# Reciprocals taken on 128x8 and spread by ScalarE, with the attention's loads and copies stated later

## The chip, the cores and the metric

The kernel runs on one core of a Trainium2 chip. The metric is device time in microseconds (us) of one execution. Five engines work from instruction queues of their own, each in the order in which its queue stands: TensorE (PE, with its weight loads listed apart as PEld), VectorE (DVE), ScalarE (ACT), GpSimd (POOL) and SyncE (SP), which here only issues transfers (DMAs). An instruction whose inputs are not ready holds up everything behind it on its engine.

## The reference

```python
scores = scale * q @ k.T                       # per batch and head, 576 x 576
scores = where(causal, -1e9, scores); scores -= scores.max(-1)
a = exp(scores); a /= a.sum(-1) + 1e-09
local = a @ v
q_p = where(q > 0, q, exp(q) - 1) + 1
mem_out = (q_p @ M_prev) / (q_p @ z_prev + 1e-06)
g = 1 / (1 + exp(-beta))
x = g * mem_out + (1 - g) * local              # 4 batches x 8 heads x 576 x 64
x = x.transpose(0, 2, 1, 3).reshape(2304, 512)
r = relu(x @ w_in); x = (s * r * r + b) @ w_out          # 512 -> 2048 -> 512
h = x @ w2_in; z = h * softmax(h)                         # 512 -> 1024
x = (z - mean(z)) / sqrt(var(z) + 1e-06) * g_ln @ w2_out  # 1024 -> 512
```

The results are float32. The four weight matrices arrive as 64-bit floats, which the kernel reads as pairs of 32-bit words and "decodes" on the chip into a high and a low part.

## The kernel before, in words

The attention runs over 16 units `u` (4 batches x 4 pairs of heads). A unit has 4 full tiles of 128 query rows for each of the two heads and one shared tail tile, 9 tiles in 5 steps `i` (0 to 4; `CF` is 4). `scores` multiplies on PE, a DVE instruction (L336, L362) adds the mask, takes the row's minimum of the scaled scores (`mx`) and copies the tile to `pr`; ACT takes the exponential (L312) and sums the row into `sums`. Two steps later `transposes` turns `pr` over on PE (tiles `pp`, L377), and ACT copies it to `pt` (L383). `values` multiplies with `v` into the PSUM tile `po` (L411), adds the memory part `mq` x `Mb` (L416), and DVE scales `po` by `R` into `xb` (L418).

The division by the row sums is done by `weigh` and `recip_t`: the 8 row sums of a unit (4 tiles x 2 heads, a 128x8 tile) get 1e-9 added (L279); DVE takes the reciprocal of each, 64 times over, into `r` of 128x512 (L281); PE transposes `r` in four pieces (`tr`, L293), and ACT copies the result to `R` (L295). The product of `den` and `sums` (L283) weighs the memory part `ph`.

From unit 4 on the scores use a high and a low part: `split` makes `hi` of `kq` on ACT (L242, one buffer), the remainder on POOL (L243, in place), and eight copies by DMA put both into `sk` and `k2` (L249, L250). `load` brings in `kq`, `q`, `v` (two buffers each) and, at the first pair of a batch, `zb` and `Mb`. All these DMAs, the weights' loads (L147) and the stores stand in SP's one queue.

PE's spare time in the attention is filled with the first part of the MLP of finished batches (`first_part`, L430 to L432 and L471 to L473), and 11 weights are decoded meanwhile: ACT L152, DVE L153, L154, L156, L158, POOL L159, ACT L163, DVE L164. After the attention come the rest of that first part, the second part (`second_part`) and the second MLP (`mlp2`).

Nobody writes the order of the queues by hand. A scheduler lays out the queues from the order in which the program states its instructions: what is stated earlier goes first where two could go, and its own model of times decides when something could. To state a load or a copy later in the program is thus to give it a lower rank against what stands between.

Of the kernel before, what the change touches and what calls it, by code (L numbers as in the profile page):

```python
# [8 lines left out]
F32 = mybir.dt.float32  # L9
# [3 lines left out]
AF = mybir.ActivationFunctionType  # L13
# [4 lines left out]
P = 128  # L18
# [5 lines left out]
def attention_mlp_kernel(  # L24
# [9 lines left out]
    nc = tc.nc  # L34
    B, NPAIR, _, NCH, _, D = q.shape
    H = 2 * NPAIR
# [7 lines left out]
    CF = S // P  # L44
# [31 lines left out]
    def warm_up(n):  # L76

        ps = ps_m.tile([P, 512], F32, tag="m", name=f"warm{n}")
        for _ in range(n):
            nc.tensor.matmul(ps[:, 0:256], warm[:, 0:P], warm, start=True, stop=True)  # L80

    def load_gate():
        nc.sync.dma_start(gate, beta.partition_broadcast(P))
        nc.scalar.activation(gate, gate, AF.Exp, scale=-1.0)
        nc.vector.tensor_scalar(gate, gate, 1.0, None, ALU.add)
        nc.vector.reciprocal(gate, gate)
        nc.vector.tensor_scalar(omg, gate, -1.0, 1.0, ALU.mult, ALU.add)
        gg = gate.rearrange("p (a j) -> p a j", j=2)
        nc.vector.tensor_copy(gmt[0:64], gg[0:64, :, 0])
        nc.vector.tensor_copy(gmt[64:128], gg[64:128, :, 1])  # L90

    def load_consts():
        nc.sync.dma_start(s_sb, moe_s.partition_broadcast(P))
        nc.sync.dma_start(b_sb, moe_b.partition_broadcast(P))
        with nc.allow_non_contiguous_dma(reason="a small vector"):
            nc.sync.dma_start(gl_sb, g_ln.rearrange("(f p) -> p f", p=P))
# [78 lines left out]
    def decode_to(n):  # L175
        while decoded[0] < min(n, NW):
            with tc.issue_after(mark[0]) if mark[0] else nullcontext():
                decode(decoded[0])
            decoded[0] += 1


    NU = B * NPAIR

    QT = S + CF * P
    RL = QT + P
    NRAW = NPAIR
    xbs = {}

    class Attention:
# [16 lines left out]
            self.zb = {}  # L206
            self.tiles = [(i, j) for i in range(CF) for j in range(2)] + [(CF, None)]

        def load(self, u, names=("kq", "q", "v")):
            b, a = divmod(u, NPAIR)  # L210
            p = self.pair.setdefault(u, {})
            if "kq" in names:
                t = p["raw"] = self.ld.tile([P, RL], F32, tag="kq", name=f"kq{u}")
                nc.sync.dma_start(t, kq[b, a])
            for nm in "qv":
                if nm in names:
                    t = p[nm] = self.ld.tile([P, NCH, 2, D], F32, tag=nm, name=f"{nm}{u}")
                    nc.sync.dma_start(t, (q if nm == "q" else v)[b, a])
            if a == 0 and "v" in names:
                self.zb[b] = self.st.tile([P, H, D], F32, tag="zb", name=f"zb{b}", bufs=1)  # L220
                nc.sync.dma_start(self.zb[b], z_prev[b].partition_broadcast(P))
                for j in range(2):
                    nc.sync.dma_start(self.Mb[b % 2][j * D:(j + 1) * D, :, j * D:(j + 1) * D],
                                      M_prev[b].rearrange("(a j) d e -> j d a e", j=2)[j])

        def gates(self, u):

# [45 lines left out]
        def weigh(self, u):  # L273


            p = self.pair[u]
            sums, den, ph = p.pop("sums"), p.pop("den"), p["ph"]
            sv = sums[:, 0:CF].rearrange("p c h -> p (c h)")
            nc.vector.tensor_scalar(sv, sv, 1e-9, None, ALU.add)  # L279
            r = p["r"] = self.st.tile([P, CF * 2, D], F32, tag="r", name=f"r{u}", bufs=1)  # L280
            nc.vector.reciprocal(r, sv.unsqueeze(2).to_broadcast([P, CF * 2, D]))  # L281
            dv = den.rearrange("p c h -> p (c h)")
            nc.vector.tensor_tensor(dv, dv, sums.rearrange("p c h -> p (c h)"), ALU.mult)  # L283
            nc.gpsimd.tensor_tensor(ph.rearrange("p c h d -> p (c h) d"), ph.rearrange("p c h d -> p (c h) d"),
                                    dv.unsqueeze(2).to_broadcast([P, NCH * 2, D]), ALU.mult)

# [197 lines left out]
    def load2(bi, part=None):  # L484
        t0, n = blocks[bi]
        if part is not True:
            x = xq[bi] = xs2.tile([P, NC, NB], F32, tag="x", name=f"xr{bi}")
            nc.sync.dma_start(x[:, :, 0:n], xd[:, :, t0:t0 + n])
        if part is not False:
            nc.sync.dma_start(yT[:, :, t0:t0 + n], yd[:, :, t0:t0 + n])  # L490

    pctx = ctx.enter_context(ExitStack())
    with ExitStack() as fctx:
        xp = fctx.enter_context(tc.tile_pool(name="xp", bufs=2))
        xs = fctx.enter_context(tc.tile_pool(name="xs", bufs=1))
        gs = fctx.enter_context(tc.tile_pool(name="gs", bufs=FP1 + 1))
        ys = fctx.enter_context(tc.tile_pool(name="ys", bufs=2))
        ps_m = fctx.enter_context(tc.tile_pool(name="ps_m", bufs=2, space=PSUM))
        fpools = [xs, gs, ys, [ps_m]]
        filler = []  # L500
        with ExitStack() as actx:
            at = Attention(actx, xp)
            NS = CF + 1
            G = NU * NS
            at.load(0, ("kq",))
            warm_up(16)
            load_gate()
            at.load(1, ("kq",))
            at.load(0, ("q", "v"))
            at.phi(0)  # L510
            at.load(1, ("q", "v"))
            load_consts()
            LAG = 2
            FG = NPAIR * NS + LAG + 1
            debt = 0.0
            tiles_of = lambda i: (2 * i, 2 * i + 1) if i < CF else (2 * CF,)
            for g in range(G + LAG):
                u, i = divmod(g, NS)
                if g < G:
                    for t in tiles_of(i):  # L520
                        at.scores(u, t)
                if g < 4:
                    with tc.issue_after(at.last):
                        warm_up(6)
                if i == 0 and NRAW <= u + 1 < NU:
                    at.split(u + 1)
                if i == 0 and u + 2 < NU:
                    at.load(u + 2)
                if i == 2 and 0 < u < NU:
                    at.phi(u)  # L530
                if i == 3 and u < NU:
                    at.gates(u)
                if i == CF and u < NU:
                    at.weigh(u)
                if 0 <= g - LAG:
                    lu, li = divmod(g - LAG, NS)
                    for t in tiles_of(li):
                        at.transposes(lu, t)
                    if li == CF - 1:
                        at.recip_t(lu)  # L540
                        at.phi_t(lu)
                    if li == CF:
                        at.values(lu)
                        if lu % NPAIR == NPAIR - 1:
                            filler.append(first_part(lu // NPAIR, fpools))
                decode_to(min(int(g / 3.4), RA))
                if filler and g >= FG:
                    debt += 0.93 * 6 * (FP1 + NC) / (G - FG)
                    while debt >= 1 and filler:
                        debt -= 1  # L550
                        if next(filler[0], 0) == 0:
                            filler.pop(0)
        wpools[1] = ctx.enter_context(tc.tile_pool(name="wpB", bufs=RB, side="right", reuse_waits="tile"))
        xs2 = pctx.enter_context(tc.tile_pool(name="xs2", bufs=1, side="right", reuse_waits="tile"))
        gs2 = pctx.enter_context(tc.tile_pool(name="gs2", bufs=2, side="right", reuse_waits="tile"))
        ps_y = pctx.enter_context(tc.tile_pool(name="ps_y", bufs=1, side="right", space=PSUM, reuse_waits="tile"))
        ps_h = pctx.enter_context(tc.tile_pool(name="ps_h", bufs=2, side="right", space=PSUM, reuse_waits="tile"))
        fpools[3] = [ps_h, ps_m]
        load2(0, False)
        attended[0] = True  # L560
        for it in filler:
            for _ in it:
                decode_to(min(decoded[0] + 1, RA + RB))
# [198 lines left out]
```

## Time and profile before

| what | value |
|---|---|
| median of 3 runs | 941.71 us (938.75 to 942.41) |
| profiled execution, own time | 937.02 us |
| its span (what the rows cover) | 935.2 us |
| PE busy | 876.7 us (94%) |
| DVE busy | 627.6 us (67%) |
| ACT busy | 453.0 us (48%) |
| POOL busy | 217.3 us (23%) |
| mean granted PE clock | 0.983 of full speed |

Busy shares are averages over stages that differ: the attention takes about the first 384 us, the rest of the first part and the second part follow to some 600 us, then the second MLP. PE's busy time counts a pipelined matmul from its start to a modelled end, so a PE that is busy is not always at its peak; PEld gives the weight loads beside it.

### The profile page before, as it was taken

How to read it: one execution, taken by the hardware profiler on the slowest of the kernel's cores; microseconds unless marked ns; L12 is line 12 of the kernel's file. 1: busy time of each engine (PE TensorE's matmuls, PEld its weight loads, DVE VectorE, ACT ScalarE, POOL GpSimd, SP SyncE). 2: the span in 40 equal slices, each digit the busy share in tenths (PEclk: the TensorE clock that was granted, in tenths of full speed). 3: DMA queues.
4: the chain of work that ended last, by engine and by line, in shares of the span. 5: the costliest groups of instructions: out<-in, count | busy, mean ns of one | idle time of the engine just before them, and what ended most of it. 6: DMA issues, size and time to landing. Idle time of an engine off the chain costs nothing.

```text
span 935.2 us, 13612 instructions
## 1 busy us (share of the span) xinstructions
PE 876.7 (94%) x5008; PEld 706.2 (76%) x5008; DVE 627.6 (67%) x1251; ACT 453.0 (48%) x1008; POOL 217.3 (23%) x176
## 2 busy tenths in 40 slices
PE   8897878899999899799989999999999999999997
PEld 5444655887887787698767888889877888888886
DVE  5977899677676867699897633243898645444442
ACT  4665676556666666455345332233443533333332
POOL 5334435233333322143340300000232100000000
PEclk9989799999999999999999999999999999999999
DMA  8339757565656550345833200010140000000000
GB/s 241 101 112 245 199 152 182 152 186 153 179 133 182 130 135 13 112 161 158 305 106 98 90 6 18 1 46 2 45 136 23 12 23 23 22 23 23 23 23 34
DMA packets 46530, 93.69 MB, mean 100 GB/s; under 512 B 7808, under 2 KB 21120, under 8 KB 46464
## 3 DMA queue, kind: packets, MB, share of 16 engines
q1 hardware_dynamic: 46464, 92.83, 34.4%
q8 instruction: 39, 0.64, 0.3%
q14 instruction: 27, 0.22, 0.1%
HBM read 56.63 MB, written 14.16 MB: 76 GB/s over the span
## 4 chain that ended last, share of the span: by engine, by line
PE 61%; DVE 17%; DMA 9%; issue 5%; ACT 3%; SPq 3%; POOL 1%; ACTq 0%; DVEq 0%; POOLq 0%
PE h L430 5%; PE h L432 5%; PE h L431 4%; PE h L634 4%; PE h L636 4%; PE h L635 3%; PE o L694 3%; PE o L693 3%; PE o L692 3%; PE y L595 3%; PE y L593 3%; PE y L594 3%; PE pp L377 3%; PE po L411 3%; DMA k<-hi 2%
## 5 line engine op out<-in xcount | busy, mean ns | idle before, releaser
L159 POOL TENSOR_TENSOR wa<-wa,raw 128x512 f32<-128x512 f32 x48 | 83.6, 1748 | 279.7 <-DVE raw L158 263.9
L430 PE MATMUL h<-xh,w 128*128 128x512 f32 (+2 forms) x380 | 129.8, 346 | 8.0 <-ACT r L433 3.0
L432 PE MATMUL h<-xh,w 128*128 128x512 f32 (+2 forms) x380 | 129.5, 341 | 0.9 <-DVE w L164 0.8
L431 PE MATMUL h<-xl,w 128*128 128x512 f32 (+2 forms) x380 | 129.4, 341 | 0.1
L434 DVE SCALAR_TENSOR_TENSOR r<-r,s_sb 128x512 f32<-128x512 f32 (+2 forms) x95 | 80.7, 855 | 61.3 <-ACT r L433 60.7
L312 ACT ACTIVATE pr<-pr,mx 128x128 f32<-128x128 f32 (+2 forms) x144 | 83.4, 580 | 38.8 <-DVE mx L336 29.4
L433 ACT ACTIVATE r<-h 128x512 f32<-128x512 f32 (+2 forms) x95 | 45.8, 487 | 90.0 <-PE h L432 83.9
L430 PEld LDWEIGHTS h<-xh,w 128*128 128x128 f32 x380 | 71.7, 190 | 20.7 <-ACT r L433 3.9
L593 PE MATMUL y<-gh,w 128*128 128x512 f32 (+1 forms) x220 | 81.7, 376 | 3.5 <-ACT gh L435 3.3
L594 PE MATMUL y<-gh,w 128*128 128x512 f32 (+1 forms) x220 | 81.3, 374 | 0.0
L432 PEld LDWEIGHTS h<-xh,w 128*128 128x128 f32 x380 | 71.7, 189 | 9.6 <-DVE w L164 1.8
L431 PEld LDWEIGHTS h<-xl,w 128*128 128x128 f32 x380 | 71.8, 189 | 8.0 <-DVE xl L443 0.9
L336 DVE CUSTOM_DVE_ANT_0 pr<-s,big 128x128 f32<-128x128 f32 (+3 forms) x128 | 60.2, 481 | 23.6 <-PE s L330 16.9
L595 PE MATMUL y<-gl,w 128*128 128x512 f32 (+1 forms) x220 | 68.2, 373 | 5.1 <-DVE gl L438 5.1
L383 ACT ACTIVATE pt<-pp 128x128 f32<-128x128 f32 (+3 forms) x128 | 51.7, 431 | 31.4 <-PE pp L377 31.1
L377 PE MATMUL pp<-ident,pr 128*128 128x128 f32 x384 | 62.9, 284 | 4.1 <-DVE xb L419 1.1
L411 PE MATMUL po<-pt,v 128*64 128x256 f32 (+1 forms) x384 | 61.2, 357 | 2.1 <-ACT pt L383 1.9
L438 DVE SCALAR_TENSOR_TENSOR gl<-r,b_sb,gh 128x512 fp32r<-128x512 f32 (+1 forms) x55 | 44.8, 816 | 23.1 <-ACT gh L435 21.0
L377 PEld LDWEIGHTS pp<-ident,pr 128*128 128x128 f32 x384 | 46.8, 147 | 16.1 <-issue 5.8
L435 ACT ACTIVATE gh<-r,b_sb 128x512 fp32r<-128x512 f32 (+1 forms) x55 | 37.2, 678 | 42.9 <-DVE r L434 30.7
L692 PE MATMUL o<-w,zh 128*128 128x512 f32 x144 | 56.3, 391 | 0.9 <-ACT zh L686 0.9
L694 PE MATMUL o<-w,zl 128*128 128x512 f32 x144 | 56.3, 391 | 0.6 <-DVE zl L687 0.6
(137 smaller groups left out, 2057.3 us busy)
## 6 DMA issues: line engine op xcount, KB each, us to landing
raw<-in_moe_w_in_dram SPq DMA_DIRECT2D x24, 512.0 KB, 4.1
raw<-in_moe_w_out_dram SPq DMA_DIRECT2D x24, 512.0 KB, 3.5
kq<-in_kq_dram SPq DMA_DIRECT2D x16, 608.0 KB, 3.9
sk<-hi SPq DMA_DIRECT2D x24, 304.0 KB, 5.0
sk<-kq SPq DMA_DIRECT2D x24, 304.0 KB, 4.9
q<-in_q_dram SPq DMA_DIRECT2D x16, 320.0 KB, 4.5
v<-in_v_dram SPq DMA_DIRECT2D x16, 320.0 KB, 3.8
xd<-xb SPq DMA_DIRECT2D x4, 1152.0 KB, 6.0
```

The lines of the kernel that those rows point to most:

```text
L159: nc.gpsimd.tensor_tensor(a, a, lf, ALU.add)
L312: mark[0] = nc.scalar.activation(pr, pr, AF.Exp, bias=mx, scale=-1.0, accum_out=sm).ins
L377: nc.tensor.transpose(pp[:, c * P:(c + 1) * P], pr[:, c * P:(c + 1) * P], ident)
L411: nc.tensor.matmul(o, vr[:, c, j], m, start=(cp == 0 and c == 0), stop=False)
L430: nc.tensor.matmul(ps, wc[0], xh[:, c, 0:n], start=(c == 0), stop=False)
L431: nc.tensor.matmul(ps, wc[0], xl[:, c, 0:n], start=False, stop=False)
L432: nc.tensor.matmul(ps, wc[1], xh[:, c, 0:n], start=False, stop=(c == NC - 1))
L593: nc.tensor.matmul(o, wc[0], gh[:, 0:n], start=(f == fs[0]), stop=False)
L594: nc.tensor.matmul(o, wc[1], gh[:, 0:n], start=False, stop=False)
L595: nc.tensor.matmul(o, wc[0], gl[:, 0:n], start=False, stop=(f == fs[-1]))
L692: nc.tensor.matmul(oo, zh, w[:, 0], start=(f == 0), stop=False)
L694: nc.tensor.matmul(oo, zl, w[:, 0], start=False, stop=(f == NF2 - 1))
```

## The change

Two things are edited. First, `weigh` takes the reciprocals on the 128x8 tile itself, in place, and ACT spreads each over 64 columns into `r` with one copy (128x512); the product for `den` is taken before, since `sums` is overwritten. Second, the loads are stated one by one at other steps: `kq` of `u + 2` at step 4 (units 0 to 3) or step 2 instead of step 0, `q` at step 3, `zb` and `Mb` of `u + 1` at step 3, and `v` of `u + 2` right behind `values` of `u`; `split(u + 1)` moves from step 0 to step 1. The amount of data and every matmul stay as they are.

```diff
@@ weigh
             sv = sums[:, 0:CF].rearrange("p c h -> p (c h)")
             nc.vector.tensor_scalar(sv, sv, 1e-9, None, ALU.add)
-            r = p["r"] = self.st.tile([P, CF * 2, D], F32, tag="r", name=f"r{u}", bufs=1)
-            nc.vector.reciprocal(r, sv.unsqueeze(2).to_broadcast([P, CF * 2, D]))
             dv = den.rearrange("p c h -> p (c h)")
             nc.vector.tensor_tensor(dv, dv, sums.rearrange("p c h -> p (c h)"), ALU.mult)
+            r = p["r"] = self.st.tile([P, CF * 2, D], F32, tag="r", name=f"r{u}", bufs=1)
+            nc.vector.reciprocal(sv, sv)
+            nc.scalar.activation(r, sv.unsqueeze(2).to_broadcast([P, CF * 2, D]), AF.Copy)
@@ before the loop
-            at.load(0, ("kq",))
+            at.load(0, "kq")
             warm_up(16)
             load_gate()
-            at.load(1, ("kq",))
-            at.load(0, ("q", "v"))
+            at.load(1, "kq")
+            at.load(0, "q", "z", "v")
             at.phi(0)
-            at.load(1, ("q", "v"))
+            at.load(1, "q", "v")
@@ in the loop over steps
-                if i == 0 and NRAW <= u + 1 < NU:
+                if i == 1 and NRAW <= u + 1 < NU:
                     at.split(u + 1)
-                if i == 0 and u + 2 < NU:
-                    at.load(u + 2)
+                if i == (CF if u < NRAW else 2) and u < NU:
+                    at.load(u + 2, "kq")
+                if i == 3 and u < NU:
+                    at.load(u + 2, "q")
+                    at.load(u + 1, "z")
@@ behind the transposes of the last tile of unit lu
                         at.values(lu)
+                        at.load(lu + 2, "v")
```

The scheduler makes new queues of this. Three places follow; a number behind a tile's letter is its unit, the last number only a tag.

ScalarE at the start of unit 4, before the change:

```order
L383 ACTIVATE pt3_1_1_938<-pp3_7_982 128x4x128
L163 ACTIVATE w4_885<-wa4_878 128x512
L242 ACTIVATE hi6_1218<-kq6_970 128x1216
L312 ACTIVATE pr4_2_1005,sums4_946<-pr4_2_1005,mx_1009 128x256
L312 ACTIVATE pr4_3_1011,sums4_946<-pr4_3_1011,mx_1015 128x256
L152 ACTIVATE wa5_1059<-raw5_1057 128x512
L295 ACTIVATE R3_993<-tr3_988 128x512
L312 ACTIVATE pr4_4_1069,sums4_946<-pr4_4_1069,mx_1073 128x384
L304 ACTIVATE mq3_995<-tp3_996 128x512
```

and of the changed kernel, from the same weight (`w4`) on:

```order
L163 ACTIVATE w4_878<-wa4_871 128x512
L316 ACTIVATE pr4_0_942,sums4_948<-pr4_0_942,mx_946 128x128
L316 ACTIVATE pr4_1_950,sums4_948<-pr4_1_950,mx_954 128x128
L316 ACTIVATE pr4_2_987,sums4_948<-pr4_2_987,mx_991 128x256
L316 ACTIVATE pr4_3_993,sums4_948<-pr4_3_993,mx_997 128x256
L152 ACTIVATE wa5_1057<-raw5_1055 128x512
L316 ACTIVATE pr4_4_1067,sums4_948<-pr4_4_1067,mx_1071 128x384
L299 ACTIVATE R3_975<-tr3_970 128x512
L308 ACTIVATE mq3_977<-tp3_978 128x512
L265 ACTIVATE ph4_1083<-ph4_1083 128x640
L390 ACTIVATE ptl_137<-pp3_8_1015 128x512
L245 ACTIVATE hi6_1283<-kq6_1081 128x1216
```

`hi6`, the copy for unit 6, has moved from in front of three exponentials of unit 4 and of `R3` and `mq3` to behind all of them. Of the later ones, `hi7` and `hi8` move behind four more exponentials, `hi10` behind three, `hi11` behind two, and `hi9` and `hi12` to `hi15` behind one or none.

VectorE at the end of unit 5, before the change:

```order
L362 ISA pr5_8_1461,mx_1467<-st5_0_1462,big_63 128x288
L270 TENSOR_SCALAR den5_1376<-den5_1376 128x10
L271 RECIPROCAL den5_1376<-den5_1376 128x10
L279 TENSOR_SCALAR sums5_1208<-sums5_1208 128x8
L281 RECIPROCAL r5_1482<-sums5_1208 128x512
L283 TENSOR_TENSOR den5_1376<-den5_1376,sums5_1208 128x10
L362 ISA pr5_8_1461,mx_1474<-st5_1_1469,mtail_68,mx_1467 128x288
```

and of the changed kernel:

```order
L282 TENSOR_SCALAR sums5_1211<-sums5_1211 128x8
L340 ISA pr6_0_1545,mx_1549<-s6_0_1546,big_63 128x128
L153 TENSOR_SCALAR wa7_1435<-wa7_1435 128x512
L284 TENSOR_TENSOR den5_1377<-den5_1377,sums5_1211 128x10
L340 ISA pr6_1_1553,mx_1557<-s6_1_1554,big_63 128x128
L154 SCALAR_TENSOR_TENSOR wa7_1435<-raw7_1433,wa7_1435 128x512
L286 RECIPROCAL sums5_1211<-sums5_1211 128x8
L340 ISA pr6_2_1609,mx_1613<-s6_2_1610,big_63 128x256
```

Where the long reciprocal stood in one piece in front of the last score tile, a 128x8 one now stands four places behind the sums, past one decoding step of a weight (L154).

SyncE's queue behind the copies for unit 4, before the change:

```order
L250 DMA k2_4_754<-kq4_542 64x576
L147 DMA raw6_1161<-in_moe_w_out_dram 128x1024
L214 DMA kq5_763<-in_kq_dram 128x1216
L218 DMA v4_546<-in_v_dram 128x640
L221 DMA zb1_548<-in_z_prev_dram 128x512
L218 DMA q5_765<-in_q_dram 128x640
L214 DMA kq6_970<-in_kq_dram 128x1216
```

and of the changed kernel:

```order
L253 DMA k2_4_792<-kq4_700 64x576
L147 DMA raw6_1164<-in_moe_w_out_dram 128x1024
L221 DMA v4_838<-in_v_dram 128x640
L224 DMA zb1_895<-in_z_prev_dram 128x512
L218 DMA kq5_922<-in_kq_dram 128x1216
L221 DMA q5_893<-in_q_dram 128x640
L218 DMA kq6_1081<-in_kq_dram 128x1216
```

`v4` and `zb1` now stand in front of `kq5`; the rest of this stretch is as it was.

## Rows read from the trace of the kernel before

**Rows 1.** Five stages: start:end, length; busy PE, PEld, DVE, ACT, POOL; clock, DMA share, GB/s.

```profile
0.00:100.00 100.00, 82.13 (x458) 48.17 (x458) 73.60 (x186) 57.29 (x150) 44.78 (x48) 0.92 0.61 174
100.00:150.00 50.00, 40.12 (x280) 30.31 (x282) 48.10 (x101) 33.89 (x86) 21.39 (x16) 0.94 0.64 173
150.00:384.00 234.00, 222.35 (x1661) 181.71 (x1658) 167.84 (x403) 144.09 (x383) 74.07 (x58) 0.99 0.53 138
384.00:500.00 116.00, 105.54 (x553) 90.00 (x553) 105.20 (x166) 57.99 (x114) 38.71 (x21) 0.97 0.55 180
550.00:600.00 50.00, 50.00 (x222) 41.41 (x221) 18.26 (x26) 13.35 (x22) 0.00 (x0) 1.00 0.04 11
```

**Rows 2.** Groups by line, 0 to 384: busy, mean ns, idle before.

```profile
L281 DVE RECIPROCAL r<-sums 128x512 f32<-128x512 f32 x16 | 53.5, 3344 | 0.4
...
L242 ACT ACTIVATE hi<-kq 128x1216 fp32r<-128x1216 f32 x12 | 14.6, 1219 | 33.0 <-DMA k<-hi 19.7 <-DMA k<-kq 5.7 <-DMA sk<-hi 4.3
...
L154 DVE SCALAR_TENSOR_TENSOR wa<-raw,wa 128x512 int32<-128x512 int32 x11 | 12.3, 1125 | 0.1
...
L295 ACT ACTIVATE R<-tr 128x512 f32<-128x512 f32 x16 | 9.4, 588 | 5.4 <-PE tr L293 5.4
...
L163 ACT ACTIVATE w<-wa 128x512 fp32r<-128x512 f32 x11 | 6.9, 625 | 3.3 <-POOL wa L159 3.3
...
L271 DVE RECIPROCAL den<-den 128x10 f32<-128x10 f32 x16 | 3.4, 211 | 0.2
```

**Rows 3.** Waits of PE, 0 to 384: total, times, longest.

```profile
PE s L329 <- DVE mx L336: 8.7, 9, 2.4
```

**Rows 4.** Five short stretches, columns as in the first group.

```profile
25.00:43.75 18.75, 14.91 (x101) 9.13 (x99) 18.67 (x40) 12.08 (x33) 7.32 (x6) 1.00 0.38 125
43.75:56.25 12.50, 12.50 (x45) 5.65 (x45) 7.50 (x22) 5.42 (x15) 3.56 (x3) 0.59 0.02 3
87.50:93.75 6.25, 2.64 (x16) 1.93 (x15) 2.57 (x8) 1.88 (x5) 1.39 (x3) 1.00 1.05 239
93.75:106.25 12.50, 9.37 (x49) 7.10 (x50) 10.05 (x20) 7.61 (x21) 6.54 (x4) 0.59 0.58 177
118.75:150.00 31.25, 21.40 (x150) 14.62 (x151) 31.04 (x65) 22.21 (x56) 14.38 (x9) 1.00 0.55 147
```

**Rows 5.** Timeline of ACT and PE: start, duration, then idle before.

```profile
87.05 0.63 ACT L163 ACTIVATE w<-wa 128x512 fp32r<-128x512 f32 x1 [1.26 <-POOL wa L159]
...
92.05 1.22 ACT L242 ACTIVATE hi<-kq 128x1216 fp32r<-128x1216 f32 x1 [4.37 <-DMA k<-hi]
...
95.78 0.57 ACT L304 ACTIVATE mq<-tp 128x512 f32<-128x512 f32 x1
...
96.41 1.22 PE L416 MATMUL po<-mq,Mb 128*128 128x512 f32 x1 [6.09 <-DVE wa L153]
```

**Rows 6.** Timeline around the second unit's reciprocal.

```profile
38.22 3.29 DVE L281 RECIPROCAL r<-sums 128x512 f32<-128x512 f32 x1
...
41.66 0.63 PE L293 MATMUL tr<-ident,r 128*128 128x128 f32 x4 [0.83 <-DVE mx L336]
...
43.75 0.47 PE L432 MATMUL h<-xh,w 128*128 128x288 f32 x1 [0.83 <-DVE w L164]
```

**Rows 7.** Timeline of DVE, then of PE, 132 to 150.

```profile
134.39 3.35 DVE L281 RECIPROCAL r<-sums 128x512 f32<-128x512 f32 x1
...
144.28 3.85 DVE L154 SCALAR_TENSOR_TENSOR wa<-raw,wa 128x512 int32<-128x512 int32 x2
...
148.85 0.50 PE L329 MATMUL s<-sk 128*128 128x512 f32 x1 [2.43 <-DVE mx L336]
```

**Rows 8.** Waits of the queue of loads and copies (SPq).

```profile
SPq L218 <- DVE den L269: 32.9, 8, 15.7
...
SPq L214 <- DMA k<-kq: 28.4, 9, 4.8
SPq L249 <- PE st L357: 26.8, 8, 6.5
```

More of the change, by code (lines that the diff above doesn't have):

```diff
@@ L207, in __init__, with load @@
             self.tiles = [(i, j) for i in range(CF) for j in range(2)] + [(CF, None)]
-        def load(self, u, names=("kq", "q", "v")):
+        def load(self, u, *names):
+            if u >= NU:
+                return
             b, a = divmod(u, NPAIR)
             p = self.pair.setdefault(u, {})
[L212 to L216, printed above, removed]
+            for nm in names:
+                if nm == "kq":
+                    t = p["raw"] = self.ld.tile([P, RL], F32, tag="kq", name=f"kq{u}")
+                    nc.sync.dma_start(t, kq[b, a])
+                elif nm in "qv":
                     t = p[nm] = self.ld.tile([P, NCH, 2, D], F32, tag=nm, name=f"{nm}{u}")
                     nc.sync.dma_start(t, (q if nm == "q" else v)[b, a])
[L219 to L224, printed above, removed]
+                elif a == 0:
+                    self.zb[b] = self.st.tile([P, H, D], F32, tag="zb", name=f"zb{b}", bufs=1)
+                    nc.sync.dma_start(self.zb[b], z_prev[b].partition_broadcast(P))
+                    for j in range(2):
+                        nc.sync.dma_start(self.Mb[b % 2][j * D:(j + 1) * D, :, j * D:(j + 1) * D],
+                                          M_prev[b].rearrange("(a j) d e -> j d a e", j=2)[j])
         def gates(self, u):
```

## The prediction

> **What bounds the kernel now.** I read the profile by stages first [rows 1], then the groups of instructions of the attention [rows 2], then what TensorE (PE) waits for there [rows 3], and last the stretches and timelines in which PE stands still [rows 4 to 7]. In [rows 1] the reader should set the second number, PE's busy time, against the length. From 550 to 600 us PE is busy without a break; in the first 100 us it lacks 17.9 us, from 100 to 150 it lacks 9.9, in the 234 us after that 11.7. The work on PE is the same before and after the change, so the change can only give back such gaps and the time in which PE's clock is granted at less than full.
>
> Who makes the gaps? From 118.75 to 150 VectorE (DVE) is busy 31.04 of 31.25 us while PE has 21.40, and from 25 to 43.75 DVE is busy 18.67 of 18.75 [rows 4]: there DVE is the bound. From 150 to 384 DVE is busy 167.84 of 234 us and PE 222.35 [rows 1]: there PE is, or nearly. From 87.5 to 93.75 neither works (2.64 and 2.57 of 6.25 us), and [rows 5] show why: ScalarE (ACT) ends a copy at 87.68, then stands 4.37 us in front of `hi` (L242), whose single buffer is still being read by the copies of the unit before. Behind it in ACT's queue are the exponentials and `mq`; PE needs `mq` for L416, which starts at 96.41 after 6.09 us of standing. The row names DVE's L153, but `mq` at 95.78 is what came last. After that pause PE's granted clock is 0.59 on average over 93.75 to 106.25 [rows 4], a mixture of the levels 1.2 and 2.4 GHz, although nothing is wrong any more. The same follows the standing before 43.75: 0.59 from 43.75 to 56.25.
>
> **The change part by part.** The program's median is 941.71 us; the profiled execution took 937.02, so 4.7 less. I make the sum against 937.0 and add 4.7 at the end.
>
> The reciprocal: 16 times 3.344 us, 53.5 us, leave DVE [rows 2]. A 128x8 one is put at the 0.211 us of the 128x10 one (L271). DVE thus loses 3.13 us a unit, 50 us in all, of which only what stands in PE's way counts.
>
> (1) `hi6`. In the new order of ACT it stands behind `R3` and `mq3` instead of in front. The 6.09 us [rows 5] should go, and with them the slow clock: PE's 9.37 busy us at 0.59 cost 9.37 x 0.41 = 3.8 us [rows 4]. That is 9.9. Other `hi` remain where they wait: 19.7 us in 8 waits on this cause are in [rows 2], 2.5 on average if shared evenly, and I leave one such wait in place. Taken: 7, between 0 (the wait returns further on) and 9.9.
>
> (2) The DVE-bound stretch from 118.75 to 150 holds one reciprocal, at 134.39 [rows 7]. DVE is busy throughout, so its 3.1 us come back whole. Taken: 3, between 0 and PE's whole gap, 9.85.
>
> (3) The stretch from 25 to 43.75 holds the one at 38.22; right behind it PE stands 0.83 us before the transposes of `r` and 0.83 before a matmul that needs the weight queued behind it on DVE [rows 6]. These 1.7 go. The slow clock that follows costs 12.5 x 0.41 = 5.1 us [rows 4]; no row tells whether it goes when the standing in front of it shrinks, so I take half of it. Taken: 4, between 0 and 6.8.
>
> (4) The other 14 reciprocals: the longest waits of PE on score tiles are 8.7 us together, 9 times [rows 3], and a good part of these is in (2). From 150 to 384 PE's gap is 11.65 us. Taken: a quarter, 3, between 0 and 11.65.
>
> (5) ACT gains 16 copies of 128x512. The nearest rows are `R` at 0.588 us and the weight's copy from SBUF at 0.625 [rows 2]; the source here is in SBUF, so 0.63, 10 us in all. ACT is busy 235 of the first 384 us (the first three rows of [rows 1]), so most of it lies in idle time: while `r` is copied, PE has `po` and the next scores to do. Taken: -1, between 0 and -10. The Trainium skill speaks against the move: "ScalarE: Activation LUTs", section "Rules for kernel authors", wants simple elementwise work on VectorE and budgets some 0.3 us and 0.83 ns per element on ScalarE, an estimate of 0.73 us here, a tenth above the rows; by it the 10 us would be 11.6. It does not turn the sign, since ACT has idle time where DVE has none.
>
> (6) The loads. In the queue of SP the shift is a place or two (`v4` before `kq5`). Waits there are long, 32.9, 28.4 and 26.8 us [rows 8], but of PE's waits up to 384 us none names a load of `kq`, `q` or `v`; what the load waits for is a buffer, and that comes free when it did. Cost nothing, under cover of two buffers each; if the cover goes, a late `sk` holds PE at the next unit's first score. Stating `split` later is what moves `hi`, counted in (1).
>
> (7) The new order has waits of its own. The decode of the three weights 7 to 9 still sits among the score tiles of unit 6: before, two L154 took 3.85 us on DVE and PE stood 2.43 us for the tile behind [rows 7]. More decode steps now stand in front of that tile. Taken: -1, between 0 and -4.
>
> Sum: 7 + 3 + 4 + 3 - 1 - 1 = 15. From 384 us on nothing is touched; the same number of matmuls of the first part (672) stands in PE's queue before the attention's last one in both orders. 937.0 - 15 = 922 for the profiled execution, 927 by the median.
>
> **The rivals.** *Covered anyway.* PE is busy 95% of 150 to 384, the order of before was laid out with the long reciprocal in view and has matmuls beside it, and the loads hardly move. Then only (1) or (3) come through, a gain of up to 8: about 938. For it: DVE does not fill this stretch. Against it: the two saturated stretches of [rows 4]. Chance 0.22.
>
> *More than counted.* PEld, the weight loads, is busy 41.41 of 50 us where PE is dense, 82.8%, but 60.6% from 100 to 150 and 77.7% from 150 to 384 [rows 1]. By that ratio the two stretches hold 50 x (1 - 60.6/82.8) = 13.4 and 234 x (1 - 77.7/82.8) = 14.4 us of slack, 27.8 where busy time shows 21.5. If a freer DVE gives all of it back, with 5.1 and 1.7 of (3): 34.6, so 907; with the first 100 us tightened as well, some 900. The Trainium skill ("Perfetto Trace Analysis", section "Identifying Performance Opportunities") holds matmul busy share a poor measure and wants weight-load busy share; [rows 4] agree that busy is not fast, with 12.50 of 12.50 us busy at a clock of 0.59. Against it: many loads of the attention are of 64 columns and shorter, so the ratio exaggerates. Chance 0.12.
>
> *ACT held at `r`: slower.* ACT now waits for DVE's small reciprocal, and in unit 5 a decoding step (L154, 1.125 us on average [rows 2]) stands between the sums and it on DVE. Queued behind `r` on ACT are the exponentials of the next unit and the copies of `pp`, for which PE waits. If a unit loses 0.5 + 1.125 us to this, 16 units lose 26, against the 15 counted: 952 or so by the median. It decides from about 0.94 us a unit (15/16). Against it: ACT has 39% idle in these 384 us, and in most units the small reciprocal stands only one or two short steps behind the sums. Chance 0.08.
>
> **How the numbers follow.** The forecast itself, a gain of 8 to 27, has 0.58; its time is 927. A measurement of this kernel tells from no change about 0.5%, 4.7 us. Faster by more: 0.58 + 0.12 and 0.06 of the covered case, 0.76; within 0.5%: the other 0.16 of it; slower: 0.08. The low end, 907, is the first price of "more than counted" and leaves out about half of it, 0.06; the high end, 943, holds the covered case and leaves out the slower one and a little, 0.10. The likeliest case alone spans 915 to 934.
>
> **What would show it.** (1) no 4 us pause of ACT before `hi6`, PE not idle around 90 us, clock full there. (2), (4) DVE some 50 us less busy, 16 reciprocals near 0.2 us; DVE no longer full from 119 to 150. (3) the clock after the second unit. (5) 16 copies near 0.63 us and no exponential waiting long behind one. (6) POOL still waiting on `v`, PE on no load. The attention's last matmul near 369 us instead of 384, and the stages behind it as long as before. The prediction is wrong if a pause at another `hi` or at the three weights' decode grows by as much as (1) gives, or if the second half of the attention shrinks by more than 1 us a unit.

## The result and the profile after

The changed kernel takes 908.17 us (median of 4 runs, 902.94 to 910.94), the kernel before on the same chip 940.34. The ratio is 0.965 [0.9595, 0.9705]: faster by 3.5%, some 32 us, where 15 were forecast. A second measurement gave 907.77 and 0.967 [0.9625, 0.9714].

The profiled execution took 910.94 us, its span is 909.2. By stages the changed kernel shows (columns as in [rows 1]; the last line is the attention from the end of the sixth unit on):

```profile
0.00:100.00 100.00, 92.04 (x535) 55.85 (x536) 71.08 (x207) 67.10 (x175) 47.66 (x51) 0.91 0.64 186
100.00:150.00 50.00, 42.18 (x284) 32.05 (x284) 43.86 (x109) 34.98 (x92) 23.89 (x20) 0.93 0.81 209
523.60:573.60 50.00, 50.00 (x222) 41.43 (x222) 18.25 (x26) 13.62 (x22) 0.00 (x0) 1.00 0.04 11
...
140.00:357.60 217.60, 214.48 (x1639) 180.67 (x1638) 133.53 (x399) 146.31 (x389) 71.11 (x56) 0.99 0.56 145
```

and the kernel before in the stretch that answers to the last line (150.56 is where DVE starts to scale unit 5's `po`, 140.0 in the changed kernel):

```profile
150.56:383.70 233.14, 221.49 (x1649) 180.90 (x1646) 167.28 (x402) 144.03 (x382) 73.89 (x58) 0.99 0.54 139
```

The attention's last matmul and all work behind it tell where the gain ends: it ran at 383.56 before, and now

```profile
357.42 0.44 PE L421 MATMUL pe<-mq,Mb 128*128 128x64 f32 x2
```

That is 26.1 us sooner. The dense stage (523.6 to 573.6, 26.4 us earlier than in [rows 1]) is as it was, and the spans end 26.0 apart. So the whole gain lies in the attention: 10.6 us up to unit 5 (150.56 to 140.0) and 15.5 behind it (233.1 to 217.6). Look at PEld in the two long lines: 180.90 and 180.67 us, the same work, in 233.1 and 217.6 us of time. PE's gaps shrank there by 8.5 us (11.65 to 3.12); the other 7 were inside its busy time.

The two profiles are 26 us apart and the medians 32, since the profiled execution of the kernel before (937.02) was quicker than its four timed ones and this one the slowest of its four. Part of that is the start: the first 25 us were granted 1.00 of the full clock in the profile before and 0.80 here, and unit 0's scaling starts at 28.2 and 32.0. A second profile of the changed kernel (`after_5r`, granted 1.00 there; its line stands at the end) has unit 0's scaling at 27.5, unit 5's at 135.0 and the attention's last matmul at 351.8. With like starts the gain is thus 15.5 us up to unit 5 and 16.3 behind it.

What the edit does by itself is as forecast. In the groups from 0 to 384 us, DVE's and ACT's:

```profile
L286 DVE RECIPROCAL sums<-sums 128x8 f32<-128x8 f32 x16 | 3.2, 199 | 0.3
...
L245 ACT ACTIVATE hi<-kq 128x1216 fp32r<-128x1216 f32 x12 | 14.6, 1218 | 18.8 <-DMA k<-hi 11.3 <-DMA k<-kq 3.7 <-DMA sk<-hi 2.5
L287 ACT ACTIVATE r<-sums 128x512 f32<-128x512 f32 x16 | 10.0, 626 | 0.8 <-DVE sums L286 0.8
```

3.344 us became 0.199 (0.211 was taken), the spread costs 0.626 (0.63), and ACT waits for the small reciprocals 0.8 us in all. `hi` still waits 18.8 us where it waited 33.0 [rows 2]. The place of [rows 5] in the changed kernel:

```profile
88.55 1.22 ACT L245 ACTIVATE hi<-kq 128x1216 fp32r<-128x1216 f32 x1 [0.37 <-DMA k<-hi]
...
87.13 1.13 PE L420 MATMUL po<-mq,Mb 128*128 128x512 f32 x2 [0.19 <-ACT mq L308]
```

The pauses of 4.37 and 6.09 us are gone (0.37 and 0.19 now), as term (1) said; whether they went for its reason is a question for the runs below.

### The profile page after: what moved, and what is told of

It reads as the page before. It is cut to its first block, busy times and chain, and to the rows that moved or that the text cites. A ratio compares the mean times of both kernels' runs of the same rounds, so it can differ in the third digit from the quotient of the medians.

```text
span 909.2 us, 13596 instructions
## 1 busy us (share of the span) xinstructions
PE 872.0 (96%) x5008; PEld 708.0 (78%) x5008; DVE 578.8 (64%) x1251; ACT 458.8 (50%) x1024; POOL 214.4 (24%) x176
## 4 chain that ended last, share of the span: by engine, by line
PE 70%; DVE 17%; DMA 5%; issue 4%; ACT 2%; SPq 1%; POOL 0%; ACTq 0%; DVEq 0%; POOLq 0%
PE h L434 5%; PE po L415 5%; PE h L435 5%; PE h L436 5%; PE pp L381 4%; PE h L642 4%; PE h L643 4%; PE h L644 4%; PE y L603 4%; PE o L702 3%; PE o L701 3%; PE o L700 3%; PE y L602 3%; PE y L601 3%; DVE wa L154 3%
## 5 line engine op out<-in xcount | busy, mean ns | idle before, releaser
L438 DVE SCALAR_TENSOR_TENSOR r<-r,s_sb 128x512 f32<-128x512 f32 (+2 forms) x95 | 75.5, 799 | 64.9 <-ACT r L437 64.4
```

## The experiments

Each time is a median; the ratio compares a kernel's runs with those of the kernel before on the same chip, and is what counts where it differs from the quotient of the medians.

### Which edit it is

`recip_alone` has only the new `weigh`; `loads_alone` is the changed kernel with the old `weigh`; `split1_alone` is the kernel before with this alone:

```diff
-                if i == 0 and NRAW <= u + 1 < NU:
+                if i == 1 and NRAW <= u + 1 < NU:
```

> The kernel before with the edit of the reciprocals alone: 128x8 on VectorE, spread by ScalarE; loads and split stated as before. Theory A (VectorE's 3.1 us a unit pace the whole attention, each unit waits for it, not only the two full stretches): 20 to 30 us under the kernel before, so 910 to 920. Theory B (the gain is that of the loads and of split, hi6 above all): no more than 10 us under it, 930 or above.

> The changed kernel with the long reciprocal on VectorE put back: loads and split stated late, weigh as before. Theory A: 0 to 8 us under the kernel before (only the 7 us of hi6), 932 to 941. Theory B: 20 to 30 us under it, 910 to 920.

> The kernel before with one edit: the copy into the high part stated at step 1 instead of step 0; loads and reciprocal as before. The loads and this step together, with the long reciprocal, took 13 us off (929.2). If the step alone is what moves the copy for unit 6 behind the exponentials and takes away the 4.4 us pause with the slow clock behind it (9.9 us by the prediction's term 1), this run takes 925 to 935; if the order of the loads is needed for it, or does it, 937 to 945.

| kernel | us | ratio to before |
|---|---|---|
| recip_alone | 909.78 | 0.966 [0.9623, 0.9697] |
| loads_alone | 929.19 | 0.9859 [0.9817, 0.99] |
| split1_alone | 939.01 | 0.9988 [0.9953, 1.0023] |

The reciprocal edit alone gives the whole gain. The loads with the split give 13 us by themselves, and nothing that can be measured beside it. The split alone gives nothing, and in its profile it does not even move `hi6`, which still stands in front of the exponentials, `R3` and `mq3` and waits 4.13 us; L416 waits 5.85.

### Is it the time on VectorE, and does ScalarE's part cost anything

`cheap_b` puts a multiplication by 1 in the place of the reciprocal, on the same engine, tile and line, and so leaves out the division:

```diff
-            nc.vector.reciprocal(r, sv.unsqueeze(2).to_broadcast([P, CF * 2, D]))
+            nc.vector.tensor_scalar(r, sv.unsqueeze(2).to_broadcast([P, CF * 2, D]), 1.0, None, ALU.mult)
```

`dve_spread` (and `spread_5r`, the same kernel) is the changed kernel with the spread on VectorE, `recip_dve` has this without the loads' edits:

```diff
-            nc.scalar.activation(r, sv.unsqueeze(2).to_broadcast([P, CF * 2, D]), AF.Copy)
+            nc.vector.tensor_copy(r, sv.unsqueeze(2).to_broadcast([P, CF * 2, D]))
```

> The kernel before with the 128x512 reciprocal replaced by a 128x512 multiplication by 1 on VectorE, so the division by the row sums is left out; nothing is given to ScalarE. Theory A: as recip_alone or a few us under it, 905 to 920, VectorE's new instruction near 0.5 us. If the work given to ScalarE costs what was counted (1 us and up to 10), this kernel is 1 to 10 us faster than recip_alone. Theory B: 930 or above.

> The changed kernel with the copy that spreads the 128x8 reciprocals put on VectorE instead of ScalarE (some 0.5 us a unit there). Theory A: within 5 us of the changed kernel, 905 to 915, a little slower if VectorE paces every unit (16 x 0.5 = 8 us at most), a little faster if ScalarE does. Theory B: the same as the changed kernel.

> The kernel before with the reciprocal taken on 128x8 and spread over 64 columns by VectorE itself; loads and split as before, nothing left out. By the runs so far the loads add nothing once the reciprocal is short and the spread on VectorE costs no more than on ScalarE: 902 to 909. If the loads' edits are needed beside the spread on VectorE (904.70 with them): 910 to 916.

> The changed kernel itself once more, as the partner of the next run: 905 to 910.

> The changed kernel with the spread over 64 columns made by VectorE (a copy of 128x512 there instead of on ScalarE), nothing left out. If term (5) holds (ScalarE's copies lie in its idle time and cost 1 us) and VectorE is no longer short of time: within 2 us of the partner. If the copies on ScalarE hold up the exponentials behind them: 3 to 5 us below it.

| kernel | us | ratio to before |
|---|---|---|
| cheap_b | 905.05 | 0.9603 [0.9559, 0.9646] |
| dve_spread | 904.70 | 0.9603 [0.9565, 0.9641] |
| recip_dve | 907.18 | 0.9632 [0.9579, 0.9684] |
| after_5r, the changed kernel | 907.77 | 0.967 [0.9625, 0.9714] |
| spread_5r | 905.71 | 0.9642 [0.9606, 0.9678] |

One instruction that is short instead of long, nothing else stated differently, gives 37 us. The spread on VectorE was 2 to 4 us the better in each of three pairs (`dve_spread` and `spread_5r` against the changed kernel, `recip_dve` against `recip_alone`), and `cheap_b`, which gives ScalarE nothing, is 4.7 us under `recip_alone`. All these intervals overlap: ScalarE's copies cost 2 to 5 us, if anything.

### Its time, or the order that the scheduler makes of it

`cheap_b` differs from the kernel before in two ways: the instruction takes 0.46 us instead of 3.34, and the scheduler, whose model of times sees that, lays out all queues anew. To part the two, an edge of issue order without a wait was set between every two neighbours of each queue, so that one kernel runs in the other's order (the code is shortened):

```diff
+    for names in order.values():
+        for x, y in zip(names, names[1:]):
+            tc.add_manual_dep(by[y], x, NoSync)
```

`short_oldorder` is `cheap_b` in the order of the kernel before, `long_neworder` the kernel before in the order of `cheap_b`, `early_oldorder` the first with the long reciprocal from unit 5 on.

> The 128x512 reciprocal is replaced by a multiplication by 1 on the same engine, tile and place (the division is left out), and every engine's queue is held, instruction by instruction, in the order of the kernel before. So only the time that VectorE spends on it changes. Theory 'VectorE's time': each unit waits for it, in gaps and in TensorE's busy time alike; the whole gain comes without a new order: 905 to 915, as with the same multiplication in its own order (905.05). Theory 'the new order': a scheduler that sees a short instruction spreads the filler matmuls of the first part (48 to 93 per unit from unit 4 on before, none in unit 15) so that the last units get some; without that only the gaps that the prediction counted come back, 15 us: 920 to 927.

> The counterpart: the reciprocal stays on 128x512 (3.3 us each), and every engine's queue is held in the order that the scheduler made for the multiplication by 1. Theory 'VectorE's time': no gain, 935 to 945, or slower, since this order was laid out for a short instruction. Theory 'the new order': its share of the gain comes though the instruction is as long as before: 920 to 930. If both shares are real and add up, the gains of this run and of the one before add to the 37 us of the multiplication in its own order.

> As the first run (order of the kernel before held, division left out), but only units 0 to 4 have the short multiplication; units 5 to 15 keep the 128x512 reciprocal. The prediction's terms (1) to (3) are all in these units: 14 us by them, so 928 if they were sized rightly and the rest of its gap was missed in the later units. If the first run gains over 25 us and this one under 12, the missing part is the 'other reciprocals' of term (4), which were put at 3 us; if this one alone gains over 20, the two early stretches were undersized.

| | order of the kernel before | order laid out for the short one |
|---|---|---|
| long reciprocal | 940.6, the kernel before | 929.31, 0.9864 [0.9801, 0.9927] |
| short multiplication | 929.25, 0.989 [0.9861, 0.9918] | 905.05, 0.9603 [0.9559, 0.9646] |

`early_oldorder` took 933.76, 0.9949 [0.9915, 0.9984]: 4.8 us, for the reciprocals of units 0 to 4. Its expectation counts term (2) among these by mistake; the reciprocal at 134.39 [rows 7] is unit 5's, so that (3) and four of the fourteen of (4) lie in these units, and (2) and the other ten in the rest. The two ratios leave 5.5 us to that rest, the profiles less. From unit 0's scaling to unit 5's the kernel before takes 122.3 us, `early_oldorder` 116.1 and `short_oldorder` 114.8; from there to unit 15's they take 232.4, 232.5 and 231.5. So in the old order the later units gain next to nothing.

The shorter time alone gives 10.3 us (1.1% of 940.6), the order alone 12.8, both 37: some 14 us, 7 to 22 by the three intervals together, appear only where both come together. Neither theory is right alone. Where these 14 lie, the stretch from unit 3's scaling to unit 14's shows (columns as in [rows 1]). The kernel before:

```profile
99.38:367.65 268.27, 248.06 (x1817) 202.10 (x1816) 206.68 (x479) 170.15 (x447) 93.28 (x72) 0.98 0.58 153
```

`short_oldorder`, then `long_neworder`, then `cheap_b`:

```profile
92.85:359.83 266.98, 249.44 (x1817) 203.43 (x1816) 176.62 (x479) 168.68 (x447) 92.36 (x72) 0.97 0.59 153
```

```profile
94.74:362.50 267.76, 243.64 (x1780) 201.20 (x1781) 204.84 (x477) 167.15 (x447) 96.42 (x73) 0.97 0.62 161
```

```profile
85.65:338.00 252.35, 237.83 (x1780) 199.10 (x1781) 171.05 (x478) 168.60 (x447) 97.47 (x73) 0.97 0.65 171
```

Read the second number of each, the length: 268.3, 267.0, 267.8, 252.4. In the held order DVE is 30 us less busy here (206.7 to 176.6) and the stretch is 1.3 us shorter; with the new order and the long reciprocal it is 0.5 shorter; with both 15.9. Up to there each does something by itself: unit 3's scaling starts at 99.38, 92.85, 94.74 and 85.65. These starts hold the granted clock of the first 25 us too, 1.00 in the first two profiles and 0.80 in the others; counted from unit 0's scaling they are 71.2, 65.1, 57.7 and 54.2 us. Nearly all that the new order gives beside the long reciprocal is thus gained before unit 3's scaling.

### The pause in front of hi6, by itself

In the held order one instruction was moved on ScalarE, `hi6` from in front of three exponentials, `R3` and `mq3` to right behind `mq3` (`hi6_moved`; with the multiplication `short_hi6_moved`):

```diff
 L163 ACTIVATE w4<-wa4
-L242 ACTIVATE hi6<-kq6
 L312 ACTIVATE pr4_2
 L312 ACTIVATE pr4_3
...
 L304 ACTIVATE mq3<-tp3
+L242 ACTIVATE hi6<-kq6
```

In `hi6_both` and `short_hi6_both` POOL's remainder of `kq6` (L243) also moves, from in front of the tail tile's step `pr3_8` (L368) to behind it.

> The kernel before, every queue held in its own order, with one instruction moved on ScalarE: the copy hi6 goes from in front of three exponentials of unit 4, R3 and mq3 to right behind mq3. The reciprocal stays on 128x512. This is term (1) of the prediction by itself. Theory 'pause': the 6.09 us that TensorE stands and the slow clock behind it (3.8 us) go, 930 to 933. Rival 'returns': the wait comes back as a later hi6, whose copies into sk and k2 then hold TensorE at the scores of unit 6 or in SyncE's queue: 936 to 941.

> The same one move, with the short multiplication in place of the reciprocal in all units (the division is left out) and the order of the kernel before held: the kernel that took 929.25, plus the move. Theory 'pause': the order's share of the gain is mostly this pause: 917 to 922, about 10 us below. Theory 'filler': it is in the later units; the move gives what it gives with the long reciprocal or less, 925 to 930.

> The kernel before, order held, 128x512 reciprocal kept, with two instructions moved: the copy hi6 on ScalarE behind mq3, as in the run before, and on POOL the remainder of kq6 from in front of the tail tile's step of unit 3 (pr3_8) to behind it. Theory 'two queues held one pause': now the 6 us of standing go and unit 3 is done 5 to 10 us sooner, 930 to 936. Rival 'something third takes its place' or 'the next stretch, full on VectorE, takes it back': 937 to 942.

> The same two moves with the short multiplication (division left out) in the held order, which alone took 929.25. Theory 'two queues': 919 to 925. Rival: 927 to 936, as with the one move (935.87).

| kernel | us | ratio to before |
|---|---|---|
| hi6_moved | 938.57 | 1.0002 [0.997, 1.0034] |
| hi6_both | 936.57 | 0.9948 [0.9919, 0.9977] |
| short_hi6_moved | 935.87 | 0.9941 [0.9907, 0.9974] |
| short_hi6_both | 933.22 | 0.9917 [0.9882, 0.9952] |

The move on ScalarE gives nothing. The timelines of `hi6_moved` (ACT, PE, then POOL) show why:

```profile
92.97 1.22 ACT L242 ACTIVATE hi<-kq 128x1216 fp32r<-128x1216 f32 x1 [2.07 <-DMA k<-hi]
...
90.95 1.12 PE L416 MATMUL po<-mq,Mb 128*128 128x512 f32 x2 [0.55 <-ACT mq L304]
98.36 1.12 PE L377 MATMUL pp<-ident,pr 128*128 128x128 f32 x4 [6.29 <-POOL pr L368]
...
94.26 2.75 POOL L243 TENSOR_TENSOR kq<-kq,hi 128x1216 fp32r<-128x1216 f32 x1 [5.69 <-ACT hi L242]
96.98 1.32 POOL L368 TENSOR_SCALAR pr<-pr,sm 128x576 f32<-128x576 f32 x1
```

L416 no longer waits 6.09 us but 0.55; the next matmul, the transpose of the tail tile, waits 6.29 instead and starts at 98.36, where it started at 98.28 before (unit 0's scaling is at 28.3 and 28.2). POOL stands in front of `kq6`, which needs `hi6`, with the tail tile behind it. Two queues held one pause. With POOL's step moved as well (`hi6_both`) L416 waits as little, and the transposes do not wait for POOL, but the products with the tail tile now wait for VectorE (PE, DVE, PE):

```profile
98.60 1.12 PE L416 MATMUL po<-mq,Mb 128*128 128x512 f32 x2 [0.55 <-ACT mq L304]
...
100.32 3.31 DVE L263 SCALAR_TENSOR_TENSOR ph<-q,ph 128x640 f32<-128x640 f32 x1
...
104.48 0.48 PE L414 MATMUL pe<-ptl,v 128*64 128x64 f32 x4 [2.68 <-DVE ptl L389]
```

That kernel is faster by 0.5%, 4.9 us by its runs, within 2 and 8. In its profile little of this comes from the pause: unit 3's scaling follows unit 0's by 70.6 us, as against 71.2 before. The moved remainder (L243, on POOL from 99.74 to 102.95) now runs beside VectorE's L263, which takes 3.31 us where it took 0.82 before (2.85 in `hi6_moved`) and stands in front of unit 3's scaling and of the tail tile's last copy (L389). VectorE is busy 11.79 of the 12 us from 93 to 105, so the rival of the expectation, a next stretch full on VectorE that takes the gain back, holds in part. With the short instruction a third place appears (`short_hi6_both`, PE):

```profile
91.97 1.12 PE L414 MATMUL pe<-ptl,v 128*64 128x64 f32 x16 [3.54 <-ACT ptl L386]
```

`ptl`, the copy of the tail tile, stands behind `hi6` on ScalarE, and `hi6` again waits for the copies of the unit before. Both short kernels with moves are no faster than `short_oldorder` without. The order made for the changed kernel has `ptl`, `mq3` and `R3` all in front of `hi6`, and so has that of `recip_alone`, where the split is stated as before: the short reciprocal moves `hi6`, not the later split. No run clears all three places and nothing else.

### What in the order carries the rest

Three kernels have the short multiplication and a free scheduler with one rule each (edges of the same kind). `short_fill_old` holds every filler matmul of the first part in its old unit; `short_nonfill_old` holds TensorE's attention matmuls in their old order among themselves; `short_po_old` only demands that from unit 3 on each product with `v` (`po`) stands no later against the next unit's scores than before.

> Short multiplication (the division is left out), the scheduler free, but every filler matmul of the first part held in the unit in which it stands in the kernel before (0, 6, 6, 6, 48, 6, 87, 93, 76, 64, 73, 33, 66, 60, 48, 0 by unit, as against 24 in the last one when free, which took 905.05). Theory 'filler': most of what the order gave is lost, 918 to 928. Theory 'pause' or 'order of the attention itself': the spread of the filler does not matter, 903 to 910.

> Short multiplication (the division is left out), but TensorE's own attention matmuls (scores, transposes, values) held among themselves in the order of the kernel before up to the last unit; filler, the other engines and the loads are laid out anew. Theory 'order of the attention on TensorE': the gain of the order is lost, 922 to 930. Theory 'pause' (ScalarE's and SyncE's order) or 'filler': it stays, 905 to 912.

> Short multiplication (division left out), scheduler free (905.05), with one rule from unit 3 on: each product with v of a unit stands no later against the next unit's scores than in the kernel before (half of them behind 1 to 3 scores of the next unit, as against 4). Theory 'the next unit's scores must go first': 918 to 928, as when all of TensorE's attention matmuls were held (923.64). Rival 'another part of the order': 903 to 912.

How many of the next unit's eight score tiles stand in front of the middle one of a unit's products with `v`, counted in TensorE's queue and summed over 15 units, is given beside the times:

| kernel | us | ratio to before | next scores in front |
|---|---|---|---|
| before | 940.7 | 1 | 27 |
| short_oldorder, the same order | 929.25 | 0.989 [0.9861, 0.9918] | 27 |
| long_neworder, the order of cheap_b | 929.31 | 0.9864 [0.9801, 0.9927] | 56 |
| loads_alone | 929.19 | 0.9859 [0.9817, 0.99] | 22 |
| short_po_old | 928.0 | 0.9859 [0.9811, 0.9906] | 33 |
| short_nonfill_old | 923.64 | 0.9832 [0.9791, 0.9873] | 27 |
| short_fill_old | 904.70 | 0.9633 [0.9591, 0.9675] | 57 |
| cheap_b | 905.05 | 0.9603 [0.9559, 0.9646] | 56 |
| changed kernel | 908.17 | 0.965 [0.9595, 0.9705] | 61 |

My theory of the filler falls: with it where it was, nothing is lost. With the old order of the attention on TensorE half of the gain is lost, with the products held early two thirds. The stretch from unit 3 to unit 14, first of `short_fill_old`, then of `short_po_old`:

```profile
81.20:336.30 255.10, 243.61 (x1811) 201.09 (x1812) 178.22 (x483) 170.65 (x453) 96.96 (x73) 0.99 0.65 169
```

```profile
81.74:355.01 273.27, 251.19 (x1782) 202.99 (x1783) 180.21 (x476) 170.43 (x447) 97.46 (x73) 0.95 0.61 158
```

255.1 against 273.3 us, with the same start. `short_fill_old` has the filler per unit of the kernel before, so it can be set beside `short_oldorder` matmul for matmul: 12 us less, 6.0 of them PE's gaps (17.5 to 11.5) and 5.8 its busy time, which the granted clock accounts for as far as its two digits tell: 249.4 x 0.97 and 243.6 x 0.99 are both 241 to 242. Fewer gaps came with less slow clock. The gain thus needs the new order of the attention's matmuls on TensorE, on top of a short instruction on VectorE: `long_neworder` has the 56 of `cheap_b` and gains nothing in this stretch. That within this order it is the next unit's scores in front of the products with `v` is what the counts and `short_po_old` point to. It is not shown alone, since under the rule of `short_po_old` the scheduler also moved transposes of `ph` and of the weight.

## Why the prediction was wrong

The direction and the mechanism held: VectorE's long reciprocal was the cost. The size failed, at one step of the sum. **Term (4)**, "the other 14 reciprocals: a quarter, 3, between 0 and 11.65", stands for the attention from 150 us on. It measured 15.5, above its own upper end, and the prediction's own sign of being wrong came true with it: the ten units from there on shrank by 1.5 us each, where more than 1 was to tell against it.

Two things were wrong in it. First, the price was that of a shorter instruction in the order of before. As that price 3 us was not too little: in the profile of `short_oldorder` the units from 5 to 15 take 231.5 us where they took 232.4. But the new queues were read only at three places and only for what they might cost. The argument of "covered anyway", that the old order has matmuls laid beside the long reciprocal, was true, as the 267.0 against 268.3 show, and is likely what made the new order worth so much: a scheduler that no longer has to cover it puts the next unit's scores in front.

Second, PE's gap is no upper end. 7 of the 15.5 us were busy time. The rival "more than counted", put at 0.12, had the right ruler: weight loads busy 77.7% where dense stretches have 82.8% [rows 1], 14.4 us from 150 on, 907 us in all. That its total came so near is in part luck, since up to 150 it counted 20.2 us (13.4 and 6.8) where 15.5 came with like starts. After the change the share is 180.67 of 217.6 us, 83.0%. The Trainium skill ("Perfetto Trace Analysis", section "Identifying Performance Opportunities") asks for this share in the place of matmul busy time; the trace agrees with it, and my objection, that short loads exaggerate it, did not hold in this stretch.

The other terms. **(1)** to **(3)** and **(7)**: 13 were forecast up to unit 5; 10.6 came in the pair of profiles first shown, 15.5 with like starts, so that this part was sized nearly right, though no run gives each term. Within it (1) was right in its place and wrong in its reason: `split1_alone` does not move `hi6`, moving `hi6` on ScalarE alone is worth 0, and with POOL's step it is 4.9 by the medians, of which 0.6 show at unit 3 in the profile. In the changed order all three places are clear; that this is what ended the pause is likely, but not tested by itself. (3), with four of the other reciprocals: 4 was forecast, and `early_oldorder` gives 4.8 for the first five units. **(5)**, 1 us: 2 to 5, if anything; the 0.73 us set beside it lies a sixth above the 0.626 measured, not a tenth. **(6)**, the loads at nothing: right beside the short reciprocal, wrong by 13 us beside the long one, and since `split1_alone` gives nothing, that gain needs the loads' new places. "Covered" and "ACT held at `r`" did not come: ACT waited 0.8 us for the reciprocals, and none of PE's waits up to 384 us is longer than 2.5 us now.

Still open is why, inside a unit, early scores pay only with the short instruction, and what shortened PE's busy time by 7 us from unit 5 on, where the granted clock is 0.99 before and after.

## What to carry to other kernels

Where a scheduler lays out the queues by its own times, a shorter instruction is two changes: its time and a new order; price the time in the old order as the floor, and look in the new queues for what may now go first, not only for what may now wait. Measure the room on TensorE by the weight loads' share against a dense stretch of the same kernel, not by its gaps alone; in the long stretch here the share gave 14.4 us, the gaps 11.65, and 15.5 came. Before a pause is booked as a gain, follow every queue in which something stands behind the late instruction: here three queue places held TensorE to the same moment, clearing one gave nothing, and clearing two brought POOL's step beside one on VectorE that then took 2.5 us longer.

## What the runs showed of the hardware that was not expected

Spreading the 128x8 tile over 128x512 on VectorE took 0.954 us on average as a copy (`dve_spread`) and 0.464 as a multiplication by 1 (`cheap_b`). The kind of instruction is not what differs. Of the 16 copies, five ran while POOL did nothing and took 0.41 to 0.43 us; the other eleven began while POOL was in a product of two tensors and took 0.60 to 1.44. From the timelines of `dve_spread`, DVE, then POOL:

```profile
121.36 0.41 DVE L287 COPY r<-sums 128x512 f32<-128x512 f32 x1
...
141.66 1.41 DVE L287 COPY r<-sums 128x512 f32<-128x512 f32 x1
...
141.53 1.26 POOL L288 TENSOR_TENSOR ph<-ph,den 128x640 f32<-128x640 f32 x1 [2.80 <-DVE den L284]
```

The second copy ends at 143.07, 0.28 us behind POOL's product. The multiplications do the same: in `cheap_b` 15 of 16 take 0.42 or 0.43 us, and one, begun beside a product on POOL, 1.04; in `short_oldorder` the average of 0.614 comes from two of 16, above all from one that starts at 76.73 beside POOL's L243 (76.26 to 79.03), takes 2.58 and ends, too, 0.28 us behind it. L263 in `hi6_both`, shown above, ran long in the same way. The new `weigh` takes the product for `den` first, which releases POOL's L288 just before the copy: eight of the eleven began inside it.

The first 25 us were granted 0.80 of the full clock in the profile of the changed kernel shown above, and 1.00 in another of the same kernel:

```profile
0.00:25.00 25.00, 23.01 (x129) 14.02 (x129) 12.48 (x51) 14.85 (x41) 12.73 (x24) 1.00 0.75 225
```

That execution's span was 901.3 us instead of 909.2. Unit 0's scaling starts at 27.5 us there and at 32.0 in the other. A few us between two profiles of this kernel can thus come from its start alone, so that stretches from unit 3 on and the timed medians compare better than whole spans.
